# Joined 512-column matmuls, renumbered lags, idle matmuls at the start and a new order of operations in a one-core kernel

## The chip, the cores and the metric

The kernel runs on one core of one Trainium2 chip. The metric is the device time of one execution in microseconds (us). It is given as the median of several runs, with the range beside it. A profile is one of these executions; its span is about 2 us shorter than the device time of the same run. PE is the matmul engine, PEld its weight load, DVE the vector engine, ACT the scalar engine, POOL the general one, and SP the engine that issues most transfers. A line of a profile names an engine, a line of the kernel (L996), the operation and the tiles.

## The reference, cut to what matters

```python
def reference(A_u, ..., B_w_gate, B_w_up, B_w_down):      # u: 1 x 2048 x 512, bf16
    xn = layernorm(A_u)
    # A: per channel a kernel K of 2048 lags, as a sum over 128 modes, then a long convolution
    P = exp(dt * A * l)                                   # 512 channels x 128 modes x 2048 lags
    K = einsum("dn,dnl,dn->dl", C, P, dt * B).real
    y = irfft(rfft(pad(xn)) * rfft(pad(K)))[:L] + xn * Dskip
    # B: a gated network, 512 -> 1792 -> 512
    b = (sigmoid(xn @ w_gate) * (xn @ w_up)) @ w_down
    return A_u + y + b
```

The kernel takes the Fourier transforms apart into small matmuls. A table of 41 "lags" (powers of the complex modes) per channel quarter is made on DVE; matmuls turn it into K. A first stage transforms the input, a forward spectrum stage and a kernel spectrum stage follow, DVE multiplies the two spectra, and an inverse stage gives v, which is stored in DRAM. Then v is read back in another layout, and a last stage, S2, finishes the inverse transform. The gated network's matmuls run between all that.

## The kernel before

A list `ORDER` of 982 numbers fixes the order of all operations; each engine takes its own in that order. These are the parts that the change touches. The table's operations work on adjacent or on every second lag:

```python
powers(9, 2, 1, 2, 4, 3, [1, "3", "5"])       # results at lags 9, 11, 13, 15 from 1, 3, 5, 7
squares(10, 2, 5, 1, 3, ["5", "6"])
powers(17, 1, 2, 2, 7, 8, [2, 4, 8, "6", "10"])
powers(24, 2, 16, 2, 4, 9, [16, "17"])
# ... (cut)
def f_b():    # second half of a complex multiplication: L738, L739
    V.tensor_tensor(out=outp[:, :, :, 0, :], in0=outp[:, :, :, 0, :], in1=tb()[:, :, :, 1, :], op=opr)
    V.tensor_tensor(out=outp[:, :, :, 1, :], in0=outp[:, :, :, 1, :], in1=tb()[:, :, :, 0, :], op=opi)
```

The idle matmuls, whose results nobody reads, and the inverse stage (L939; the forward one, L898, is built alike), with two channel halves of DW = 256:

```python
keep_warm(14, -10)
for n in range(3):
    keep_warm(2, 1000 + n)
# ...
def fv(u=u, sv=sv, pp=pp, pq=pq):
    for y in range(2):
        src = ...                              # two or four operands
        for n, (z, q) in enumerate(src):
            for g in range(2):
                for b in (0, 64):
                    o = b ^ 64 * g
                    T.matmul(two(sv)[o:o + 64, DW * (2 * g + y):DW * (2 * g + y) + DW], mab[...],
                             z[b:b + 64, DW * g:DW * g + DW], ...)
```

And the end: the loads of v and S2. In each partition one tile t of one half p takes 2 KB, and the halves lie 16 KB apart:

```python
vps = [[at(16 * KB * p + 2 * KB * t, [2, 2, DW]) for t in range(8)] for p in range(NP)]
for t in range(8):
    for p in range(NP):
        lds.append(dma("SP" if p == 0 or t % 2 == 0 else "ACT", vps[p][t], v_v[:, :, 2 * t:2 * t + 2, :], ...))

def s2_mm(t, r, o, start, ps=(0, 1)):
    i = 2 * t + r
    for p in ps:
        for j in range(2):
            T.matmul(o[:, DW * p:DW * p + DW], s2[:, j, :], vps[p][t][:, j, r, :], ...)      # L996
        if i >= 12:
            T.matmul(o[:, DW * p:DW * p + DW], sr[:, i - 12, :], rr[:, DW * p:DW * p + DW], ...)
```

Of the kernel before, what the change touches and what calls it, by code (L numbers as in the profile page):

```python
# [13 lines left out]
ACT = mybir.ActivationFunctionType  # L14
# [22 lines left out]
NP, DW = 2, 256  # L37
# [17 lines left out]
LAG0 = (list(range(16)) + [256 + 2 * j for j in range(8)] + [768, 512, 772, 516, 776, 520, 780, 524]  # L55
        + [1024, 1280, 1288, 1792, 1800, 1536, 1544, 1032, 2048])
EXP = {6: 1, 10: 1, 12: 3, 14: 1, 19: 1, 21: 1, 22: 3, 23: 1, 27: 1, 29: 1, 31: 3, 30: 3, 37: 1, 38: 1, 39: 3}
# [117 lines left out]
def _consts():  # L175
# [30 lines left out]
UEV = (15, 19, 23, 24, 27, 28, 29, 30, 31, 32, 33, 34, 35, 36, 37, 38, 39, 40, 41, 42, 43, 44)  # L206
ON_ACT = (0,)
ORDER = [
    1, 0, 38, 28, 27, 37, 3, 4, 47, 2, 30, 29, 48, 50, 31, 49, 39, 52, 41, 51, 32, 14, 5, 7, 17, 10, 18, 6, 40, 34, 12, 42,
    33, 53, 35, 43, 44, 45, 24, 15, 94, 36, 638, 644, 93, 92, 46, 632, 54, 633, 639, 19, 105, 131, 645, 634, 95, 108, 640,  # L210
    59, 646, 685, 675, 134, 686, 132, 11, 676, 655, 656, 665, 58, 695, 670, 106, 666, 696, 96, 107, 671, 13, 16, 9, 660,
    690, 23, 677, 8, 118, 120, 119, 60, 97, 61, 98, 55, 62, 100, 691, 63, 101, 56, 678, 661, 121, 64, 680, 650, 137, 679,
    133, 21, 662, 135, 681, 651, 99, 57, 66, 672, 673, 109, 663, 635, 140, 102, 65, 67, 68, 664, 674, 179, 697, 138, 698,
    122, 636, 637, 699, 682, 667, 668, 687, 69, 20, 70, 683, 669, 684, 688, 71, 689, 149, 700, 647, 123, 110, 648, 701, 180,
    692, 72, 103, 652, 653, 22, 139, 136, 104, 111, 649, 693, 73, 124, 694, 654, 75, 113, 657, 141, 658, 150, 641, 702, 703,
    158, 642, 74, 659, 704, 728, 731, 76, 643, 181, 736, 77, 732, 227, 151, 142, 78, 127, 705, 182, 126, 183, 184, 738, 173,
    185, 739, 79, 186, 737, 706, 115, 707, 81, 80, 82, 83, 729, 733, 753, 754, 734, 708, 228, 740, 229, 230, 84, 85, 159,
    174, 175, 160, 187, 735, 87, 713, 231, 232, 86, 170, 88, 714, 125, 164, 773, 751, 90, 189, 233, 715, 112, 774, 165, 188,
    190, 166, 756, 171, 198, 192, 143, 199, 202, 200, 203, 752, 201, 755, 204, 757, 191, 206, 144, 193, 721, 167, 771, 205,
    741, 155, 772, 207, 722, 781, 172, 194, 709, 156, 145, 782, 742, 776, 152, 726, 783, 784, 777, 168, 208, 128, 114, 209,  # L220
    212, 785, 146, 723, 157, 169, 724, 727, 213, 725, 778, 779, 89, 153, 761, 763, 730, 780, 116, 764, 775, 762, 147, 129,
    154, 210, 788, 743, 91, 195, 216, 744, 214, 161, 148, 765, 758, 176, 215, 211, 745, 218, 196, 759, 760, 219, 217, 197,
    117, 234, 235, 766, 786, 177, 162, 787, 220, 222, 789, 790, 768, 716, 237, 245, 246, 236, 249, 274, 275, 250, 746, 239,
    238, 769, 767, 130, 247, 748, 770, 747, 749, 178, 163, 829, 849, 248, 276, 717, 240, 243, 750, 242, 253, 251, 241, 221,
    791, 432, 254, 433, 255, 223, 792, 402, 372, 256, 259, 224, 225, 434, 830, 226, 260, 261, 793, 244, 257, 794, 827, 403,
    373, 258, 262, 277, 438, 799, 252, 263, 850, 265, 266, 264, 404, 379, 436, 267, 374, 269, 278, 378, 408, 439, 268, 279,
    800, 283, 270, 847, 271, 280, 287, 284, 801, 281, 290, 286, 272, 292, 293, 282, 273, 440, 296, 321, 294, 297, 809, 848,
    435, 437, 371, 375, 851, 298, 828, 831, 322, 323, 857, 380, 295, 864, 441, 810, 409, 410, 300, 291, 442, 443, 301, 406,
    376, 381, 405, 377, 382, 394, 383, 395, 858, 288, 802, 285, 865, 867, 807, 396, 407, 302, 444, 303, 411, 808, 868, 289,
    387, 412, 388, 812, 817, 413, 389, 445, 424, 462, 469, 306, 832, 384, 818, 813, 391, 463, 304, 464, 837, 833, 838, 390,  # L230
    447, 392, 393, 859, 470, 385, 307, 299, 324, 819, 862, 811, 308, 860, 471, 397, 863, 398, 310, 499, 446, 468, 866, 305,
    465, 466, 386, 448, 414, 449, 467, 309, 312, 311, 313, 814, 822, 399, 415, 325, 417, 454, 400, 314, 823, 315, 820, 316,
    472, 473, 326, 861, 418, 336, 419, 331, 815, 317, 795, 327, 821, 852, 839, 455, 477, 416, 451, 452, 453, 450, 401, 484,
    425, 840, 853, 339, 328, 329, 872, 456, 426, 474, 421, 478, 854, 422, 841, 457, 340, 343, 873, 816, 458, 423, 420, 475,
    479, 476, 481, 855, 333, 824, 893, 483, 522, 480, 482, 341, 894, 332, 342, 825, 427, 335, 826, 344, 428, 485, 842, 334,
    843, 486, 459, 844, 345, 460, 347, 346, 856, 492, 898, 834, 845, 899, 835, 487, 488, 836, 803, 429, 430, 338, 523, 529,
    461, 348, 846, 349, 869, 900, 874, 524, 875, 870, 493, 489, 871, 494, 350, 876, 507, 901, 498, 527, 497, 431, 353, 895,
    905, 913, 354, 330, 318, 355, 490, 896, 351, 508, 357, 509, 491, 525, 513, 511, 512, 514, 352, 319, 337, 359, 903, 358,
    877, 356, 360, 320, 496, 526, 510, 361, 362, 363, 618, 364, 365, 528, 622, 620, 495, 369, 628, 878, 879, 366, 897, 367,
    906, 515, 953, 500, 516, 517, 880, 501, 530, 518, 604, 502, 885, 519, 531, 552, 503, 624, 553, 886, 887, 554, 532, 520,  # L240
    597, 598, 914, 559, 605, 904, 599, 954, 923, 533, 560, 888, 943, 589, 606, 561, 924, 537, 558, 534, 555, 556, 557, 562,
    563, 544, 603, 602, 538, 955, 928, 539, 535, 956, 564, 601, 600, 521, 957, 929, 545, 958, 918, 574, 607, 944, 565, 567,
    543, 504, 608, 536, 546, 542, 541, 582, 568, 540, 368, 547, 566, 959, 919, 569, 933, 934, 548, 907, 960, 908, 583, 630,
    505, 570, 571, 573, 609, 961, 584, 930, 572, 506, 931, 909, 610, 575, 576, 925, 549, 590, 962, 902, 616, 932, 586, 550,
    585, 587, 588, 611, 591, 926, 927, 577, 915, 945, 935, 578, 551, 579, 881, 592, 370, 889, 593, 580, 946, 916, 936, 937,
    594, 595, 581, 947, 950, 948, 596, 917, 612, 920, 626, 921, 949, 951, 963, 938, 952, 617, 922, 613, 625, 629, 940, 910,
    26, 941, 939, 614, 615, 619, 627, 911, 942, 631, 912, 964, 967, 710, 711, 965, 882, 712, 718, 968, 883, 966, 890, 623,
    884, 971, 969, 891, 719, 621, 804, 972, 970, 892, 796, 720, 975, 805, 797, 976, 977, 806, 798, 973, 978, 974, 25, 980,
    979, 981]
# [60 lines left out]
def kernel(  # L310
# [221 lines left out]
    keep_warm(14, -10)  # L532
    for n in range(3):
        keep_warm(2, 1000 + n)
# [4 lines left out]
    def layernorm(i0, i1, prio):  # L539
# [14 lines left out]
        for i in range(i0, i1):  # L554
# [20 lines left out]
            tr = pl.add("PE", 0.80, ft, [xn_ready[i - 1], xn_ready[i], l_id], prio, acq=[sl])  # L575
# [58 lines left out]
    q5 = pl.add("ACT", 2.15, f_sin, [q3, q4], PR, tab="sin")  # L634
# [85 lines left out]
    def cmul(lo, outp, n, m, conj, buf, deps, prio):  # L720
# [9 lines left out]
        def f_a():  # L730
            lov = wide(lo) if n == 1 or lo.ap[2][0] == 4 else lo
            ov = wide(outp) if n == 1 or outp.ap[2][0] == 4 else outp
            V.tensor_tensor(out=ov, in0=lov, in1=mre, op=ALU.mult)  # L733
            V.tensor_tensor(out=wide(tb()), in0=lov, in1=mim, op=ALU.mult)  # L734
# [5 lines left out]
        a = pl.add("DVE", 0.14 + 0.27 * n, f_a, deps, prio, acq=[sl])  # L740
        return pl.add("DVE", {1: 0.37, 2: 0.48, 4: 0.73, 7: 1.19}.get(n, 0.15 + 0.134 * n), f_b, [a], prio - 0.1, rel=[sl])
# [3 lines left out]
    for c in range(4):  # L745
# [26 lines left out]
        for dst, src in ((1, 0), (2, 1), (4, 2), (8, 3), (16, 8), (25, 9), (32, 10), (40, 11)):  # L772
            def f_s(H=H, dst=dst, src=src, c=c, ws=ws):
                S.activation(out=H[:, :, dst, :, :].rearrange("p r c h -> p c r h"),
                             in_=W[c // 2][:, src, :, ws].rearrange("p c (r h) -> p c r h", h=2), func=ACT.Identity)
            seeds[dst] = pl.add("ACT", 0.31, f_s, [W_op[src], cur_op] + hdep, PC)
# [5 lines left out]
        def powers(o0, os, l0, ls, nn, lev, need):  # L782
            h_ops[str(o0)] = cmul(H[:, :, l0:l0 + (nn - 1) * ls + 1:ls, :, :], H[:, :, o0:o0 + (nn - 1) * os + 1:os, :, :], nn,
                                  W[c // 2][:, lev, :, ws], False, "tg", dep(need) + [W_op[lev], o_g], PC - 0.5)
# [206 lines left out]
    def s2_mm(t, r, o, start, ps=(0, 1)):  # L991
        kw = dict(stop=True, skip_group_check=True)
        i = 2 * t + r
        for p in ps:
            for j in range(2):
                T.matmul(o[:, DW * p:DW * p + DW], s2[:, j, :], vps[p][t][:, j, r, :], start=start and j == 0, **kw)  # L996
# [150 lines left out]
```

## Time and profile before

| | before |
|---|---|
| time | 244.35 us, median of 3 runs (244.27 to 244.44) |
| span of the profiled run | 242.7 us |
| PE / DVE / ACT busy | 218.4 / 193.2 / 180.8 us |
| PE idle from 70 to 169 us | 6.7 us |
| last table matmuls start | 168.96 us |
| last inverse group ends | 212.54 us |

The prediction below shows the lines from which this is read. First the transfers that SP issues from 229 us on, then PE's timeline of the same stretch, then the row of PE's granted clock in 40 slices (9 is full). A timeline line has start, duration, engine, line, operation, result and operand, and the count merged into it; an idle time ahead of it would stand in brackets.

```profile
229.25 0.53 SPq L416 DMA_DIRECT2D big<-v_scr  x1
230.05 7.51 SPq L416 DMA_DIRECT2D out_dram<-big  x6
```

```profile
228.88 1.03 PE L996 MATMUL pair<-big 128*128 128x256 bf16 x8
229.75 3.19 PE L1076 MATMUL bank<-wd_sb,hT_sb 128*128 128x512 bf16 x13
232.78 1.04 PE L996 MATMUL pair<-big 128*128 128x256 bf16 x8
...
235.18 3.19 PE L1076 MATMUL bank<-wd_sb,hT_sb 128*128 128x512 bf16 x14
```

(The clock records of this profile begin at 17.50 us. What lies before the first record is counted as full, here and in every granted clock below, so a slow start doesn't show in them: twenty 256-column matmuls from 14.89 us took 180 ns each, ten from 117.62 us 109.)

### The profile page before, as it was taken

The numbers are of one execution on the slowest core, as the hardware profiler recorded it, in microseconds if no ns is written. First come the engines' busy times: TensorE is split into PE (matmuls) and PEld (weight loads), VectorE is DVE, ScalarE is ACT, GpSimd is POOL, SyncE is SP. The second block draws the span as 40 slices with busy tenths as digits, with TensorE's granted clock in tenths as the row PEclk, the third lists the DMA queues.
The fourth block names the chain that finished last, engine by engine and source line by source line (L and its number), as shares of the span: only waits on it lengthen the run. The fifth ranks groups of instructions, "written<-read, shape, count | busy, mean of one in ns | idle before, by whom it ended". The sixth has DMA issues, their size and how long they took to land.

```text
span 242.7 us, 5745 instructions
## 1 busy us (share of the span) xinstructions
PE 218.4 (90%) x2248; PEld 120.6 (50%) x2276; DVE 193.2 (80%) x397; ACT 180.8 (75%) x292; POOL 17.1 (7%) x42
## 2 busy tenths in 40 slices
PE   0099999999998999989989999999899999999994
PEld 0065444444443354555555575544564655644862
DVE  2997999999999999999999999999053246760662
ACT  3789999999999888848699999985555878440000
POOL 1303070001000020002010000000020100000000
PEclk9999999999999999999999999999999999999999
DMA  7999946501334896317975865625689798679262
GB/s 139 250 286 370 353 154 175 148 3 21 109 130 140 248 220 133 100 48 182 258 179 148 244 166 154 214 68 135 189 243 242 168 284 216 162 170 332 107 216 89
DMA packets 50861, 43.64 MB, mean 180 GB/s; under 512 B 12561, under 2 KB 44050, under 8 KB 50834
## 3 DMA queue, kind: packets, MB, share of 16 engines
q1 hardware_dynamic: 48738, 40.58, 58.8%
q0 software_dynamic: 864, 1.57, 4.1%
q10 hardware_dynamic: 1232, 1.11, 1.4%
q8 instruction: 18, 0.29, 0.5%
q14 instruction: 9, 0.07, 0.1%
HBM read 24.64 MB, written 12.06 MB: 151 GB/s over the span
## 4 chain that ended last, share of the span: by engine, by line
PE 35%; DVE 30%; ACT 23%; DMA 7%; issue 3%; SPq 1%; DVEq 0%; ACTq 0%
PE bank L1076 10%; PE bank L1028 6%; DVE big L733 5%; DVE big L734 5%; PE pair L916 5%; ACT big L666 4%; ACT big L672 4%; DVE big L739 4%; PE bank L1043 4%; DVE big L738 4%; ACT hT_sb L1037 3%; DVE hT_sb L1058 3%; ACT big L697 3%; PE pair L939 3%; ACT big L557 3%
## 5 line engine op out<-in xcount | busy, mean ns | idle before, releaser
L1028 PE MATMUL bank<-xnT,wg_sb 128*128 128x512 bf16 (+1 forms) x228 | 55.1, 375 | 2.3 <-issue 0.7
L1043 PE MATMUL bank<-xnT,wu_sb 128*128 128x512 bf16 x214 | 53.3, 379 | 2.0 <-DVE hT_sb L1058 1.1
L1076 PE MATMUL bank<-wd_sb,hT_sb 128*128 128x512 bf16 x216 | 50.3, 379 | 0.6 <-issue 0.2
L1028 PEld LDWEIGHTS <-wg_sb 128*128 128x128 bf16 x236 | 23.1, 100 | 27.4 <-issue 4.1
L1037 ACT ACTIVATE hT_sb<-bank 128x512 bf16<-128x512 f32 x56 | 32.1, 611 | 3.8 <-PE bank L1028 3.7
L1043 PEld LDWEIGHTS <-wu_sb 128*128 128x128 bf16 x224 | 21.1, 98 | 26.3 <-issue 3.4
L922 DVE TENSOR_TENSOR big<-big 128x2048 bf16<-128x2048 bf16 x16 | 19.5, 1222 | 18.3 <-PE pair L939 6.7
L1076 PEld LDWEIGHTS <-hT_sb 128*128 128x128 bf16 x224 | 21.4, 98 | 25.1 <-issue 0.4
L733 DVE TENSOR_TENSOR big<-big 128x1024 bf16<-128x1024 bf16 (+4 forms) x40 | 25.9, 647 | 0.9
L734 DVE TENSOR_TENSOR big<-big 128x1024 bf16<-128x1024 bf16 (+4 forms) x40 | 25.8, 644 | 0.0
L1058 DVE TENSOR_TENSOR hT_sb<-hT_sb,bank 128x512 bf16<-128x512 bf16 x34 | 22.4, 681 | 3.7 <-PE bank L1043 2.1
L916 PE MATMUL pair<-big 128*128 128x256 bf16 x160 | 19.8, 273 | 1.3 <-DMA big<-c_E 1.3
L918 ACT ACTIVATE big<-pair 128x1024 bf16<-128x1024 f32 x16 | 16.2, 1031 | 5.6 <-PE pair L916 5.0
L943 ACT ACTIVATE big<-pair 128x1024 bf16<-128x1024 f32 x16 | 16.4, 1035 | 4.5 <-DMA v_scr<-big 2.5
L738 DVE TENSOR_TENSOR big<-big 128x512 bf16<-128x512 bf16 (+4 forms) x40 | 18.8, 469 | 0.6
L739 DVE TENSOR_TENSOR big<-big 128x512 bf16<-128x512 bf16 (+4 forms) x40 | 18.5, 463 | 0.0
L916 PEld LDWEIGHTS <-big 128*128 128x128 bf16 x160 | 15.3, 98 | 6.0 <-DMA big<-c_E 1.6
L903 ACT ACTIVATE big<-pair 128x1024 bf16<-128x1024 f32 x16 | 16.3, 1027 | 1.7 <-PE pair L898 1.7
L697 ACT ACTIVATE big<-pair 128x1024 bf16<-128x1024 f32 x16 | 16.1, 1025 | 0.0
L790 ACT ACTIVATE sq_sb<-big 128x256 bf16<-128x256 bf16 (+2 forms) x20 | 12.7, 632 | 4.5 <-DVE big L796 3.1
L1054 ACT ACTIVATE us_sb<-bank 128x512 bf16<-128x512 f32 x22 | 13.0, 598 | 1.0 <-DVE hT_sb L1058 0.9
L666 ACT ACTIVATE big<-big 128x512 bf16<-128x512 f32 x24 | 13.8, 628 | 0.0
(106 smaller groups left out, 274.8 us busy)
## 6 DMA issues: line engine op xcount, KB each, us to landing
big<-c_E SPq DMA_DIRECT2D x16, 320.0 KB, 3.4
z_scr<-big SPq DMA_DIRECT2D x16, 256.0 KB, 2.7
big<-z_scr SPq DMA_DIRECT2D x16, 256.0 KB, 3.8
big<-big SPq DMA_DIRECT2D x64, 64.0 KB, 3.4
v_scr<-big SPq DMA_DIRECT2D x16, 256.0 KB, 3.2
big<-v_scr SPq DMA_DIRECT2D x12, 256.0 KB, 4.1
big<-in_A_u_dram SPq DMA_DIRECT2D x4, 512.0 KB, 5.8
wu_sb<-in_B_w_up_dram SPq DMA_DIRECT2D x2, 896.0 KB, 10.2
```

The costliest lines, as they stand in the source:

```text
L666: S.activation(out=W[p][:, k], in_=cur[:, :, DW * p:DW * p + DW], func=ACT.Identity)
L697: ev = pl.add("ACT", 0.90, lambda sl=sl, zs=zs: S.activation(out=zs().rearrange("p j d -> p (j d)"), in_=two(sl), func=ACT.Identity), [fx_ ...
L733: V.tensor_tensor(out=ov, in0=lov, in1=mre, op=ALU.mult)
L734: V.tensor_tensor(out=wide(tb()), in0=lov, in1=mim, op=ALU.mult)
L738: V.tensor_tensor(out=outp[:, :, :, 0, :], in0=outp[:, :, :, 0, :], in1=tb()[:, :, :, 1, :], op=opr)
L739: V.tensor_tensor(out=outp[:, :, :, 1, :], in0=outp[:, :, :, 1, :], in1=tb()[:, :, :, 0, :], op=opi)
L916: T.matmul(two(sk)[:, o:o + DW], es()[:, g, kt, :], kT[p][:, kt, :], start=kt in (0, NKT - 1), stop=kt >= NKT - 2)
L1028: T.matmul(bank(sl)[:, c0:c1], w[:, kt, k * 128:(k + 1) * 128], xnT[:, grp, kt, c0:c1], start=(kt == 0), stop=(kt == KT - 1))
L1037: S.activation(out=hT_sb[:, hs.idx, k % 2, :], in_=bank(sl), func=ACT.Sigmoid)
L1043: T.matmul(bank(sl), wu_sb[:, kt, k * 128:(k + 1) * 128], xnT[:, grp, kt, :], start=(kt == 0), stop=(kt == KT - 1))
L1058: V.tensor_tensor(out=h(), in0=h(), in1=us_sb[:, us.idx, :] if on else bank(sl), op=ALU.mult)
L1076: T.matmul(bank(po), hT_sb[:, hts[k // 2].idx, k % 2, jj * 128:(jj + 1) * 128], wd_sb[:, k, :], start=(k == 0), stop=k == FT - 1, **kw)
```

## The change

The intent: DVE writes table results to adjacent lags, short matmuls are joined into ones of 512 columns, PE is warmed up before its first real work, and the order is searched anew for these durations. The core of the diff:

```diff
-LAG0 = (list(range(16)) + [256 + 2 * j for j in range(8)] + [768, 512, ...] ...)
+LAG0 = [0, 1, 3, 5, 7, 6, 4, 2, 8, 10, 14, 12, 9, 11, 13, 15, 256, 262, ...]
-    keep_warm(14, -10)
-    for n in range(3):
-        keep_warm(2, 1000 + n)
+    warm = [keep_warm(14, -10)] + [keep_warm(4, -9 + n) for n in range(6)]
@@ (the first transposes get "+ warm" in their list of dependencies)
-        powers(9, 2, 1, 2, 4, 3, [1, "3", "5"])
-        squares(10, 2, 5, 1, 3, ["5", "6"])
-        powers(17, 1, 2, 2, 7, 8, [2, 4, 8, "6", "10"])
+        powers(12, 1, 4, 3, [1, "2", "3"])
+        squares(9, 3, 3, ["3", "5"])
+        powers(17, 5, 7, 8, [6, 7, 8, "5", "9"])
@@ (and so on: every result a run of adjacent lags)
@@ the inverse stage; the forward one likewise
-                T.matmul(two(sv)[o:o + 64, DW * (2 * g + y):DW * (2 * g + y) + DW], ...)
+                T.matmul(two(sv)[o:o + 64, DW * (2 * g + y):2 * DW * (g + 1)], ...)
@@ S2
-    vps = [[at(16 * KB * p + 2 * KB * t, [2, 2, DW]) for t in range(8)] for p in range(NP)]
+    vall = at(0, [NP, 8, 2, 2, DW])
+    vps = [[vall[:, p, t] for t in range(8)] for p in range(NP)]
-        for p in ps:
-            for j in range(2):
-                T.matmul(o[:, DW * p:DW * p + DW], s2[:, j, :], vps[p][t][:, j, r, :], ...)
+        w = slice(DW * ps[0], DW * ps[-1] + DW)
+        for j in range(2):
+            T.matmul(o[:, w], s2[:, j, :], vall[:, ps[0]:ps[-1] + 1, t, j, r, :], ...)
@@ ORDER: 985 numbers, a new sequence (cut)
@@ the estimates of durations for the search, the choice of engine for some evictions (cut)
```

## The prediction

> **What bounds the kernel now.** I read the page's busy shares first, then a table of engines by stretch, then who PE waited for, and last the timelines of PE and DVE. The page:
>
> ```profile
> PE 218.4 (90%) x2248; PEld 120.6 (50%) x2276; DVE 193.2 (80%) x397; ACT 180.8 (75%) x292; POOL 17.1 (7%) x42
> PE   0099999999998999989989999999899999999994
> DVE  2997999999999999999999999999053246760662
> ACT  3789999999999888848699999985555878440000
> ```
>
> PE does nothing in the first two slices and is near full in all others; DVE is full from slice 4 to slice 28 and slack after; ACT is full up to about 70 us. So no one engine bounds the whole. The stretches (columns: busy us of PE, PEld, DVE, ACT, POOL, then clock and DMA):
>
> ```profile
> 0.00:11.90 11.90, 0.00 (x0) 0.00 (x1) 6.91 (x25) 6.25 (x10) 2.93 (x12) 1.00 0.86 191
> 20.00:70.00 50.00, 49.55 (x226) 22.36 (x229) 47.28 (x102) 49.70 (x84) 6.29 (x13) 1.00 0.53 160
> 70.00:110.00 40.00, 36.74 (x476) 18.83 (x478) 39.31 (x87) 33.50 (x61) 1.22 (x3) 1.00 0.54 147
> 110.00:169.00 59.00, 55.57 (x746) 32.30 (x752) 58.65 (x120) 52.42 (x88) 2.44 (x6) 1.00 0.65 174
> 169.00:239.00 70.00, 68.46 (x764) 41.58 (x774) 32.52 (x48) 31.99 (x42) 2.27 (x3) 1.00 0.73 209
> ```
>
> Up to 70 us ACT (49.70 of 50) and PE are full together. From 70 to 169 us DVE is the full one (39.31 of 40, 58.65 of 59) and PE loses 3.26 + 3.43 = 6.7 us. From 169 us PE alone is full (1.5 us lost in 70). At the end there is nothing to win but PE work, since DVE and ACT are half idle; in the middle, DVE work is worth what PE loses by it. The waits of PE say how much that is:
>
> ```profile
> PE pair L573 <- DVE big L562: 11.9, 1, 11.9
> PE pair L822 <- DVE big L795: 1.7, 2, 1.2
> PE pair L916 <- DMA big<-c_E: 1.3, 1, 1.3
> PE bank L1043 <- DVE hT_sb L1058: 1.1, 1, 1.1
> PE pair L844 <- ACT big L828: 0.9, 1, 0.9
> ```
>
> 11.9 us are the start (loads and layernorm of the first tiles); of the rest, DVE table results and DVE products hold up PE most, but in small pieces. And the start on PE:
>
> ```profile
> 11.90 1.89 PE L573 MATMUL pair<-ident,big 128*128 128x128 bf16 x16 [11.90 <-DVE big L562]
> 13.58 1.06 PE L529 MATMUL bank<-glu_sb 128*128 128x512 bf16 x2
> 14.89 3.60 PE L1028 MATMUL bank<-xnT,wg_sb 128*128 128x256 bf16 x20 [0.24 <-ACT xnT L578]
> 26.53 3.19 PE L529 MATMUL bank<-glu_sb 128*128 128x512 bf16 x14
> ```
>
> Twenty 256-column matmuls take 3.6 us, 180 ns each, where 256 columns take 109 ns later (ten of L916 from 117.62 to the next start at 118.71): PE starts cold. The fourteen idle matmuls that were meant to warm it run at 26.5 us, when it has long been warm, as a filler of 3.0 us.
>
> [...] Trace: fourteen 512-column ones from 26.53 to 29.55 are 216 ns each, so joining by itself saves almost nothing. [...]
>
> ```profile
> 64.00 0.42 DVE L738 TENSOR_TENSOR big<-big 128x512 bf16<-128x512 bf16 x1
> 70.68 0.63 DVE L738 TENSOR_TENSOR big<-big 128x512 bf16<-128x512 bf16 x1
> 109.18 0.43 DVE L738 TENSOR_TENSOR big<-big 128x512 bf16<-128x512 bf16 x1
> 129.58 0.64 DVE L738 TENSOR_TENSOR big<-big 128x512 bf16<-128x512 bf16 x1
> ```
>
> 0.42 is a four-lag result with adjacent lags (the G table), 0.63 one with every second lag (the powers that start at lags 9 and 24).
>
> **The change part by part.**
>
> (1) Lags renumbered. Number and sizes of the table operations per channel quarter stay: powers of 1, 2, 4, 7, 4, 4 lags, squares of 1, 3, 3, 2, 1. Only the add/subtract halves (L738, L739) and the two instructions of each square (L795, L796) gain; the multiplies L733 and L734 take 0.69 us at 1024 elements either way. By start-to-start time of the pair L738 and L739: a power of four lags takes 1.08 us stepped (70.68 to 71.76) and 0.67 adjacent (64.00 to 64.67), so two of them save 0.82; the power of two lags, 0.39 + 0.38 us stepped against 0.30 + 0.28 adjacent in the same timeline, saves 0.19;[...] the seven-lag power was adjacent already. Sum 0.82 + 0.19 + 0.12 = 1.13 us a quarter, four quarters 4.5 us of DVE, nearly all between 67 and 169 us where DVE is full. PE loses 6.7 us in that stretch; not all to DVE (1.3 us is a DMA, 0.9 + 0.5 ACT). I take 3.0 us as shortening the whole, the rest as DVE time that PE has no idle time to give back.
>
> (2) Idle matmuls. All 38 (14 + 6 x 4) now go ahead of the first transpose, from about 1.4 us (the memset that they read ends at 0.85 + 0.52). [...] what follows runs warm. From 14.89 to 21.35 PE does 24 matmuls of 256 columns and 11 of 512, which are 24 x 0.109 + 11 x 0.216 = 5.0 us warm in 6.46 us: 1.5 us lost; the 16 transposes take 1.9 us[...]. ACT is close to full from 15 us and takes part of this back: I count 1.5 us. The fillers at 26.5 us go, but PE stood there for ACT's evictions (ACT 49.70 of 50), so nothing is counted; the two fillers at 218 us lie in the PE-bound end and free 0.4 us.
>
> (3) Joined matmuls. The inverse spectrum stage (L939) goes from 24 of 256 to 8 of 512 and 8 of 256, four array tiles at a time: 0.68 us a block now (125.06 to 125.74)[...]. The forward one (L898) goes from 8 to 4 matmuls: 0.32 us a block now (125.74 to 126.06)[...]. The last stage (L996), 64 of 256 to 32 of 512[...]. [...]I count 0.7, as the first half lies where DVE is full.
>
> (4) Order and small moves. Two tiles' statistics go to ACT instead of one (0.85 us less DVE, about 1.5 us more ACT, early where ACT is idle), one eviction fewer on ACT. The order of all 985 operations is new; it decides how much of (1) and (2) arrives. I expect it to be good, and count nothing.
>
> Sum: 3.0 + 1.5 + 0.4 + 0.7 = 5.6 us, 244.35 - 5.6 = 238.7 us.
>
> **The rivals.** (a) PE is the bound all along and DVE time is hidden: PE lost only 6.7 us in the DVE stretch, and the 70 us at the end are PE work that a faster table doesn't shorten. Then only (2) and (3) count, 2.6 us, and the time is 241.7. For it: the last 74 us are dense PE; against it: the table waits of L822 and the bank waits on DVE. (b) DVE is the bound up to 169 us and the end follows it: all 4.5 us plus the 0.85 of the statistics arrive, and the start 1 us earlier as well: 236 us. For it: DVE at 58.65 of 59; against it: work that PE doesn't do by then it must do after. (c) The idle matmuls end after the transposes are ready and hold up the whole start by 1 us, and a first weight load that lands later (the order moves the first gate piece back) adds to it: 241. For it: 38 matmuls are a fixed cost in order on PE; the first gate now waits 0.9 us for its weights. (d) The new order trades one wait for another, E-table loads or ACT evictions: 240 to 243.
>
> **Range and chances.** The middle is 238.7. Rivals (a), (c) and (d) pull up by 2 to 4 us, (b) pulls down by 3; so 235.5 to 242.3 eight times in ten. The border of 2% is 239.5, close to the middle: faster by over 2% 0.57, within 2% 0.41, slower by over 2% 0.02, as nothing added lies on PE after the start.
>
> **What would show it.** (1) L738 and L739 at 512 elements all near 0.42 us, mean of the group 0.42 to 0.45 instead of 0.53, DVE's sum down by 4 to 5 us, and the last quarter's table matmuls (L822, now from 168.96) starting 4 to 6 us earlier. (2) Idle matmuls from 1.4 to about 12 us, L1028 at 256 columns near 270 ns instead of 345 on average, the first gate near 14 us. (3) L939 blocks at 0.65 to 0.68 us, so hardly changed. (4) PE's idle time between 70 and 169 us down from 6.7 to below 4. If that idle time stays while DVE's sum falls, step (1) was worth nothing; if a new wait of over 1 us stands among PE's waits, rival (d); if the transposes start after 12.5 us waiting for PE itself, rival (c).

The sum of this forecast was 3.0 + 1.5 + 0.4 + 0.7 = 5.6 us, 244.35 to 238.7. Where the marks stand, terms and grounds are cut that no trace or run of this case shows. In step (1) the squares of three lags are 0.12 of the 1.13 us a quarter; 0.82 + 0.19 = 1.01 are from traces. In step (3) the 0.7 counted there is a bare guess. What the trace shows for it is 109 ns for a matmul of 256 columns against 216 for one of 512, so a saving of about 2 ns a pair.

## More of the kernel before

```profile
PEclk9999999999999999999999999999999999999999
```

A load of v is issued at 229.25 us, S2 runs at 232.78 us with no bracket, so PE did not stand before it, and the clock stays full to the end.

## The result, and the profile after

| | before | after |
|---|---|---|
| time, same chip | 244.39 us (244.27 to 244.57, 4 runs) | 248.03 us (247.13 to 248.68, 4 runs) |
| ratio of after to before | | 1.0146 (95% interval 1.011 to 1.0182) |
| span of the profiled run, granted clock | 242.7 us, 1.000 | 246.7 us, 0.979 |

Ratios here and below are the mean time of one kernel's fast runs over that of the other's fast runs in the same rounds, so not quite the ratio of the medians beside them. The changed kernel is 3.6 us slower, where the prediction had 5.6 us faster. It also scatters more: 1.6 us between its runs against 0.3. By the ratio it is 1.5% slower. That lies within the 2% either way to which the prediction gave 0.41, but on the side that it did not expect.

The page of the changed kernel, busy sums and rows:

```profile
PE 228.5 (93%) x2069; PEld 114.9 (47%) x2069; DVE 187.3 (76%) x397; ACT 181.5 (74%) x295; POOL 17.4 (7%) x42
PE   7959999989999998999999999999999996999492
DVE  3997999999999999999999999940635454516324
PEclk9979999999999999999999999999999999799979
```

DVE has 5.9 us less to do, as intended. PE is full for longer, yet has holes in the last seven slices, and the clock row has a 7 at three places: near 15, 210 and 235 us. The clock records behind the row show 0.50 from 15.21, 209.77 and 233.66 us, for 3.41 us each; I call that half clock. The same stretches as in the prediction (busy us of PE, PEld, DVE, ACT, POOL, then clock and DMA):

```profile
70.00:110.00 40.00, 38.55 (x536) 19.82 (x535) 39.15 (x90) 35.54 (x68) 2.47 (x6) 1.00 0.68 166
110.00:169.00 59.00, 58.51 (x780) 32.49 (x779) 52.79 (x116) 51.50 (x84) 1.76 (x4) 1.00 0.63 167
169.00:239.00 70.00, 63.54 (x438) 31.11 (x437) 30.07 (x42) 29.74 (x38) 1.73 (x2) 0.95 0.67 191
```

From 70 to 169 us PE is idle for 1.45 + 0.49 = 1.9 us instead of 6.7, and the last quarter's table matmuls start at 162.71 us, 6.2 us earlier. From 169 us on it is idle for 6.5 us instead of 1.5, at a lower clock. So the gain of the middle came, and the end lost more. The adjacent table results, by size (busy us, mean ns):

```profile
L734 DVE TENSOR_TENSOR big<-big 128x512 bf16<-128x512 bf16 x16 | 7.0, 436 | 0.1
L735 DVE TENSOR_TENSOR big<-big 128x512 bf16<-128x512 bf16 x16 | 6.9, 430 | 0.0
```

The means were 533 and 526 ns, when half of the sixteen were adjacent already. What PE now waits for (us in total, times, longest):

```profile
PE pair L992 <- DMA big<-v_scr: 4.1, 3, 3.1
PE pair L934 <- DVE big L917: 2.4, 1, 2.4
PE pair L693 <- ACT xnT L576: 1.7, 1, 1.7
...
PE bank L1024 <- DMA wg_sb<-in_B_w_gate_dram: 1.2, 1, 1.2
```

L992 is S2, L934 the inverse stage, L917 a product of spectra. Neither of the first two waits stood among the long ones of the kernel before. The end, first what SP issues, then PE:

```profile
226.92 0.52 SPq L416 DMA_DIRECT2D big<-v_scr  x1
227.54 1.79 SPq L416 DMA_DIRECT2D out_dram<-big  x2
231.34 0.53 SPq L416 DMA_DIRECT2D big<-v_scr  x1
```

```profile
226.73 3.19 PE L1072 MATMUL bank<-wd_sb,hT_sb 128*128 128x512 bf16 x14
230.27 1.04 PE L992 MATMUL pair<-big 128*128 128x512 bf16 x4 [0.36 <-DMA big<-v_scr]
234.44 1.89 PE L992 MATMUL pair<-big 128*128 128x512 bf16 x4 [3.13 <-DMA big<-v_scr]
```

Between two S2 groups of four matmuls PE stands for 3.13 us, waiting for the load that SP issued at 231.34 us. And that load had waited in turn for S2: among SP's waits from 219 us on there is one that the kernel before doesn't have.

```profile
SPq L416 <- PE pair L992: 3.2, 2, 1.9
```

That is a chain in which a load waits for a read and the next read waits for the load. By the order of the program the load of 231.34 us brings tile 0 of the second half. The two groups of S2 around it are those of tiles 4 and 2. Neither needs tile 0.

The theory that I took from this: in this kernel, the waits between reads and writes of that buffer follow the stretch of addresses from the first to the last byte that an instruction touches. The joined read of tile 2 begins at tile 2 of the first half and ends at tile 2 of the second. Tile 0 of the second half lies in between, untouched but inside. I call such a wait a false wait. The rivals: the idle start and its half clock cost most of it (1.7 + 1.2 us of waits), or joining in itself costs, as a joined group needs both halves' loads, or the new order is simply bad at the end.

### The profile page after: what moved, and what is told of

Its sections match the earlier page's. It is cut to its first block, busy times and chain, and to the rows that moved or that the text cites. A ratio compares the mean times of both kernels' runs of the same rounds, so it can differ in the third digit from the quotient of the medians.

```text
span 246.7 us, 5371 instructions
## 1 busy us (share of the span) xinstructions
PE 228.5 (93%) x2069; PEld 114.9 (47%) x2069; DVE 187.3 (76%) x397; ACT 181.5 (74%) x295; POOL 17.4 (7%) x42
## 4 chain that ended last, share of the span: by engine, by line
PE 58%; ACT 15%; DMA 13%; DVE 5%; SPq 4%; issue 2%; ACTq 1%; DVEq 0%
PE bank L1024 14%; PE bank L1039 13%; PE bank L1072 10%; PE pair L911 7%; DMA big<-v_scr 5%; PE pair L934 5%; PE pair L818 3%; ACT hT_sb L1033 3%; PE pair L992 3%; ACT big L695 3%; DMA z_scr<-big 3%; DMA wg_sb<-in_B_w_gate_dram 2%; SPq L416 2%; ACT big L664 2%; ACT big L670 2%
## 5 line engine op out<-in xcount | busy, mean ns | idle before, releaser
L1024 PE MATMUL bank<-xnT,wg_sb 128*128 128x512 bf16 (+1 forms) x236 | 56.0, 376 | 1.2 <-DMA wg_sb<-in_B_w_gate_dram 1.2
L1039 PE MATMUL bank<-xnT,wu_sb 128*128 128x512 bf16 x224 | 56.1, 384 | 0.1
L1072 PE MATMUL bank<-wd_sb,hT_sb 128*128 128x512 bf16 x224 | 51.3, 382 | 0.8 <-ACT glu_sb L1102 0.6
L1033 ACT ACTIVATE hT_sb<-bank 128x512 bf16<-128x512 f32 x56 | 33.1, 615 | 6.6 <-PE bank L1024 6.6
L1054 DVE TENSOR_TENSOR hT_sb<-hT_sb,bank 128x512 bf16<-128x512 bf16 x35 | 23.3, 680 | 9.2 <-PE bank L1039 9.1
L917 DVE TENSOR_TENSOR big<-big 128x2048 bf16<-128x2048 bf16 x16 | 19.5, 1219 | 11.9 <-DMA big<-v_scr 3.8
L938 ACT ACTIVATE big<-pair 128x1024 bf16<-128x1024 f32 x16 | 16.5, 1031 | 5.4 <-DMA v_scr<-big 3.5
L898 ACT ACTIVATE big<-pair 128x1024 bf16<-128x1024 f32 x16 | 16.4, 1032 | 4.9 <-PE pair L893 3.9
L913 ACT ACTIVATE big<-pair 128x1024 bf16<-128x1024 f32 x16 | 16.5, 1034 | 2.0 <-PE pair L911 1.2
L734 DVE TENSOR_TENSOR big<-big 128x512 bf16<-128x512 bf16 (+4 forms) x40 | 16.8, 420 | 0.2
L695 ACT ACTIVATE big<-pair 128x1024 bf16<-128x1024 f32 x16 | 16.9, 1074 | 0.0
L735 DVE TENSOR_TENSOR big<-big 128x512 bf16<-128x512 bf16 (+4 forms) x40 | 16.6, 416 | 0.0
L934 PE MATMUL pair<-big 64*64 64x512 bf16 (+1 forms) x256 | 14.1, 339 | 2.4 <-DVE big L917 2.4
L664 ACT ACTIVATE big<-big 128x512 bf16<-128x512 f32 x24 | 14.1, 654 | 0.0
L786 ACT ACTIVATE sq_sb<-big 128x256 bf16<-128x256 bf16 (+2 forms) x20 | 13.2, 663 | 1.0 <-DVE big L735 0.8
```

The source lines that it names most:

```text
L664: S.activation(out=W[p][:, k], in_=cur[:, :, DW * p:DW * p + DW], func=ACT.Identity)
L695: ev = pl.add("ACT", 0.90, lambda sl=sl, zs=zs: S.activation(out=zs().rearrange("p j d -> p (j d)"), in_=two(sl), func=ACT.Identity), [fx_ ...
L917: V.tensor_tensor(out=pp().rearrange("p q h m -> p (q h) m"), in0=xx().rearrange("p q h m -> p (q h) m"), in1=kb()[:, 0:2 * DW].unsqueeze( ...
L934: T.matmul(two(sv)[o:o + 64, DW * (2 * g + y):2 * DW * (g + 1)], mab[b:b + 64, 2 * u + g, q, :], pq()[b:b + 64, q, ch] if y else pp()[b:b ...
L1024: T.matmul(bank(sl)[:, c0:c1], w[:, kt, k * 128:(k + 1) * 128], xnT[:, grp, kt, c0:c1], start=(kt == 0), stop=(kt == KT - 1))
L1033: S.activation(out=hT_sb[:, hs.idx, k % 2, :], in_=bank(sl), func=ACT.Sigmoid)
```

## The experiments

"Before" below is always the kernel before, run beside each experiment on the same chip: 244.63 us (243.75 to 245.89, 7 runs) in the first four, 244.42 (244.15 to 246.35, 7 runs) in the second four, 244.31 (243.51 to 245.33, 11 runs) in the last four. The first four were, in the order of this section, the first four below; the second four are the tile-by-tile buffer, the two joins, the first try without idle matmuls and the bridge; the last four are the rest. Each four ran on a chip of its own. All results were correct.

### Reading the halves apart in the changed kernel

```diff
-        for j in range(2):
-            T.matmul(o[:, w], s2[:, j, :], vall[:, ps[0]:ps[-1] + 1, t, j, r, :], ...)
+        for p in ps:
+            for j in range(2):
+                T.matmul(o[:, DW * p:DW * p + DW], s2[:, j, :], vps[p][t][:, j, r, :], ...)
```

> The changed kernel with one thing undone: the last spectrum stage (S2) reads its two channel halves by separate 256-column matmuls from separate views again. Theory 1: the joined read spans both halves of the buffer, so a load of one tile's second half has to wait for matmuls of other tiles (in the program two of the last loads wait on PE; in this kernel they don't), and PE then waits for those loads: PE's waits on v_scr loads fall from 4.1 us to below 2, the half-clock window at 234 us goes, the time falls by 2 to 4 us to 244 to 246. Theory 2: the tail is late because of the order of loads and stores on the sync queue alone: no change, 247.5 to 248.5.

Measured: 242.50 us (240.76 to 243.21), ratio to before 0.9906 (0.9855 to 0.9957). Everything else of the change is still in. The same two S2 groups, now sixteen short matmuls:

```profile
226.18 3.19 PE L1071 MATMUL bank<-wd_sb,hT_sb 128*128 128x512 bf16 x14
229.20 1.91 PE L991 MATMUL pair<-big 128*128 128x256 bf16 x16
230.95 3.19 PE L1071 MATMUL bank<-wd_sb,hT_sb 128*128 128x512 bf16 x14
```

No wait between them. PE's waits for loads of v fall from 4.1 us to 1.9, one wait before the first of these groups. The joined S2 is thus worth some 5.5 us of loss (248.03 to 242.50, on two chips), more than the 2.2 us by which these waits fell. Part of the rest is half clock: in the changed kernel the four joined matmuls at 234.44 us took 1.89 us, as long as the eight at 222.84 us. The granted clock of the four runs is 0.976 to 0.982 in the changed kernel and 0.986 to 0.992 here; times the spans that is 2.7 us of lost work, my estimate. Not all of it comes from S2. The changed kernel has two half-clock stretches near the end, each of 3.41 us by the clock records. The one at 233.66 us follows S2's wait. The one at 209.77 us follows the wait for the products (L934), which is still here, 2.8 us long, but was not followed by half clock in this profile: the sixteen matmuls after it took 1.01 us, against 1.49 in the changed kernel.

### The first gate weights earlier

```diff
@@ ORDER: load 10 (first piece of the gate weights) moved ahead of load 11 (second piece)
```

> The changed kernel with one load moved in the order: the first piece of the gate weights is issued before the second piece, the S1 constant and the two tiles' parameters, instead of after them. Theory 1: in the changed kernel PE runs dry from 12.4 to 15.9 us for these weights and drops to half clock for 3.4 us from 15.2; with the weights there at 12 to 13 us, the first gate matmul starts near 14.6 us, the half-clock window there goes or moves, and the time falls by 1.5 to 3 us to 245 to 246.5. Rival: ACT is full from 15 to 70 us and sets the pace, so the earlier start is given back: less than 0.5 us.

Measured: 247.22 us (245.88 to 247.84), ratio 1.0102 (1.0057 to 1.0147). PE's wait for gate weights is gone, the wait for ACT's copy of the transposes became 2.0 us, and the half clock at 15 us stayed (the granted clock from 11.9 to 20 us is 0.79, as in the changed kernel). Some 0.8 us (1.1 by the ratios), with overlapping intervals: the late weights are not the main cause.

### All three joins in the kernel before

```diff
@@ the kernel before, with the joined forward, inverse and S2 matmuls of the change; lags, idle matmuls and order as before
```

> The kernel before with all three joined stages and nothing else. Theory 1 (joined matmuls save columns' overhead only, 0.7 us): 243.4 to 244.2. Rival (the joined S2 read adds waits between loads and matmuls of different tiles): one load waits on PE that didn't before, 244.5 to 247, with a new PE wait on v_scr loads.

Measured: 248.69 us (247.81 to 249.67), ratio 1.0171 (1.0122 to 1.0219). The joins alone make the old kernel as slow as the whole change, in an order that did not suffer before:

```profile
235.30 1.89 PE L996 MATMUL pair<-big 128*128 128x512 bf16 x4 [3.09 <-DMA big<-v_scr]
```

That is the group which ran at 232.78 us without a wait. It belongs to tile 3. Here it is the load that waits falsely. ACT issues four loads of v, the last of them the second half of tile 3, which this group does need. Before, then in this run:

```profile
219.14 3.38 ACTq L416 DMA_DIRECT2D big<-v_scr  x4
```

```profile
218.45 11.31 ACTq L416 DMA_DIRECT2D big<-v_scr  x4
```

By the trace the fourth went out at 221.90 us before. Now it goes out at 229.22, released by an S2 matmul, and lands at 235.26. The S2 group just ahead of it in the order is that of tile 5, which doesn't need tile 3, but whose stretch covers it. A half-clock stretch follows PE's wait, 234.93 to 238.34 us: the four matmuls at 235.30 us took 1.89 us, the four at 224.26 us 1.03. It is not the whole loss: the run with a granted clock of 0.998, which lost almost nothing to half clock, still took 247.81 us.

### The renumbered lags in the kernel before

```diff
@@ the kernel before, with LAG0, powers() and squares() of the change; the old order, each operation held until what it needs is issued
```

> The kernel before with the renumbered lags alone (its order kept, apart from table operations held back until what they now need is there). Prediction's step 1: DVE falls by 4 to 4.5 us and the time by 2 to 4 us, to 240.5 to 242.5. Rival (PE is the bound all along): DVE falls as much, the last quarter's table is earlier, the time stays within 1 us of 244.4.

Measured: 259.15 us over all four runs (256.53 to 261.51; two of them, over 1.5% above the fastest, count as slow), ratio 1.0518 (1.0461 to 1.0575). DVE's sum falls to 190.5 us, but PE waits for the table:

```profile
PE pair L819 <- DVE big L735: 6.1, 2, 3.2
PE pair L819 <- ACT hT_sb L1034: 2.8, 2, 1.8
PE bank L1025 <- DVE hT_sb L1055: 2.6, 1, 2.6
```

This missed its purpose. The new numbering makes the table a longer chain of results that need each other, with squares on ACT in between, and the old order blocks the engines on it: by the lists of what each result needs, the chain is 8 results deep instead of 6. That this is what costs the time is my reading of the waits. The lags have no value apart from an order made for them, so I count lags and order as one term from here on.

### The joined read over a buffer laid out tile by tile

```diff
-    vall = at(0, [NP, 8, 2, 2, DW])
-    vps = [[vall[:, p, t] for t in range(8)] for p in range(NP)]
+    vall = at(0, [8, NP, 2, 2, DW])
+    vps = [[vall[:, t, p] for t in range(8)] for p in range(NP)]
-            T.matmul(o[:, w], s2[:, j, :], vall[:, ps[0]:ps[-1] + 1, t, j, r, :], ...)
+            T.matmul(o[:, w], s2[:, j, :], vall[:, t, ps[0]:ps[-1] + 1, j, r, :], ...)
```

This is the changed kernel with the joins in, and no tile of another number between the two halves of one.

> The changed kernel with one edit: the loaded v lies tile by tile (tile, half, ...) instead of half by half, so that the joined 512-column read of a tile covers that tile's two loads only. Theory (the false waits come from the stretch of addresses that the joined read spans, not from joining): no wait of a v load on the joined matmuls, the wait of 3.1 us before the last joined group is gone, the page says full clock in the last 15 us, and the time is 241.5 to 243.0, that is as in the run with the halves read apart (242.5), within 0.5 us of it. Rival (the joined matmul itself, or the joined wait for both halves, holds up the end): a wait of over 2 us before the joined group stays, time 245 or more.

Measured: 241.90 us (241.42 to 242.73), ratio 0.9878 (0.9827 to 0.9929). What SP issues, and PE:

```profile
224.56 0.52 SPq L416 DMA_DIRECT2D big<-v_scr  x1
226.22 2.07 SPq L416 DMA_DIRECT2D out_dram<-big  x2
228.34 0.53 SPq L416 DMA_DIRECT2D big<-v_scr  x1
```

```profile
228.70 1.89 PE L992 MATMUL pair<-big 128*128 128x512 bf16 x8
230.43 3.19 PE L1072 MATMUL bank<-wd_sb,hT_sb 128*128 128x512 bf16 x14
```

S2 starts 0.36 us after the same load was issued, and these loads took 4.2 us from issue to landing (median of this page), so it cannot have waited for it. All eight joined matmuls run in one piece. SP has no wait for S2 any more. So in this kernel it is not the joining, nor the one name `vall`, which this version keeps, but the stretch of addresses that the joined read spans. That is settled by this run (241.90 us) together with the first (242.50). The runs show which waits come and go with the layout; how the waits are set was not looked at.

### Two of the joins in the kernel before

```diff
@@ the kernel before, with the joined forward and inverse matmuls; S2 as before
```

> The kernel before with the joins of the forward (four 512-column instead of eight 256-column) and inverse spectrum matmuls alone, S2 as it was. By the prediction's step 3 [...]243.4 to 244.3 against 244.4 for the kernel before. Theory (the loss of the run with all three joins, +4.1 us, is from S2 alone): not slower than before, ratio 0.996 to 1.000, no new wait at the end. Rival (joining holds banks or operands longer in these stages too): over 1 us slower, ratio above 1.004.

Measured: 244.89 us (244.46 to 246.23), ratio 1.0016 (0.9967 to 1.0065). No loss, and no gain that could be seen; the 0.7 us of the prediction are within what this doesn't tell apart from nothing.

### S2 alone joined in the kernel before

```diff
@@ the kernel before, with s2_mm() and vps of the change
```

> The kernel before with the joined S2 matmuls alone, in the half-by-half layout. Theory (all of the loss of the three joins together, 248.7, is from here): 247.5 to 249.0, a wait of about 3 us for a load of v and a half-clock window of 3.4 us behind it. Rival (the loss needs the other joins too): under 246.

Measured: 246.76 us (246.59 to 247.29), ratio 1.0095 (1.0062 to 1.0128).

```profile
231.76 1.46 PE L1077 MATMUL bank<-wd_sb,hT_sb 128*128 128x512 bf16 x6
235.39 1.04 PE L997 MATMUL pair<-big 128*128 128x512 bf16 x4 [2.17 <-DMA big<-v_scr]
```

The loss is here, 2.4 us, about the wait, but less than I expected: no half clock followed it, and the granted clock is 1.000 in all four runs. As with all three joins, ACT's load of tile 3's second half went out late, at 230.44 us. With all three joins the wait was longer, 3.09 against 2.17 us, and half clock followed it. That may be why this loss and the 0.4 us of the other two joins fall short of the 4.1 us of all three; it was not tested, and the three ran on three chips.

### Without the idle matmuls

```diff
-    warm = [keep_warm(14, -10)] + [keep_warm(4, -9 + n) for n in range(6)]
+    warm = [keep_warm(2, -10)] + [keep_warm(0, -9 + n) for n in range(6)]
```

First on the version with halves read apart:

> The changed kernel with S2's halves read apart (242.5) and 36 of its 38 idle matmuls at first taken out, two left. The prediction gave the warm start 1.5 us. Theory (the warm-up is lost in the idle 3 us after the transposes, as the half clock at 16.6 to 20.0 shows, so it gains little): 242.3 to 243.2, no more than 0.7 us slower than with the matmuls, possibly even as fast, for the transposes no longer wait for them. Rival (prediction's step 2, 1.5 us): 243.8 or more.

Measured: 244.77 us over four runs (242.23 to 246.82), ratio 0.9967 (0.9896 to 1.0039). By this my guess of at most 0.7 us was too low, but the runs were wide apart. So I ran the tile-by-tile version with and without, in five rounds:

> The tile-by-tile version again, in five rounds, as the partner of the next two: 241.4 to 242.7. Its runs differ more than those of the kernel before[...]: over 1 us between its fastest and slowest run is expected.

> The tile-by-tile version without 36 of the 38 idle matmuls at first. The first try of this on the version with halves read apart (244.8, between 242.2 and 246.8) spoke against my guess of no more than 0.7 us. If the warm start is worth the prediction's 1.5 us or more: 243.4 to 244.5. [...]within 0.7 us of the partner, 242 to 243.

Measured: with idle matmuls 242.66 us (241.52 to 244.43, 6 runs), ratio 0.9932 (0.9894 to 0.997); without 243.58 us (242.29 to 245.59, 6 runs), ratio 0.9973 (0.9934 to 1.0012). The difference is 0.9 us between the medians and 1.0 between the means of six and six runs. Worked out from these runs, its 95% interval goes from 0.5 us the other way to 2.5 us, so neither nothing nor the predicted 1.5 us is excluded, and of my two expectations neither is settled. (The second, within 0.7 us, was meant for the case that the first try's slow runs were chance.) The runs of one batch scatter more in the mended variants, by 1.3 to 4.6 us, than in the kernel before, by 0.3 to 2.2. Mostly the slower runs have the lower granted clock (tile by tile without idle matmuls from 242.29 us at 0.998 to 245.59 at 0.988), but not always: the slowest of the first four tile-by-tile runs, 242.73 us, had the highest, 0.996. Why a run falls to half clock and another doesn't was not shown. The profiles show what the idle matmuls change. In the two tile-by-tile ones the transposes start at 11.46 us with them and at 10.16 without, but the sixteen then take 2.17 us instead of 1.06, so that they end at 12.52 and 12.33 us. The start of the version with halves read apart, without them:

```profile
11.37 1.03 PE L571 MATMUL pair<-ident,big 128*128 128x128 bf16 x8 [1.07 <-DVE big L560]
14.10 1.01 PE L693 MATMUL pair<-big 128*128 128x512 bf16 x2 [1.69 <-ACT xnT L576]
16.38 6.49 PE L1023 MATMUL bank<-xnT,wg_sb 128*128 128x256 bf16 x24 [1.28 <-DMA wg_sb<-in_B_w_gate_dram]
```

And of the changed kernel, with all of them:

```profile
1.43 10.11 PE L529 MATMUL bank<-glu_sb 128*128 128x512 bf16 x38 [1.43 <-POOL glu_sb L522]
11.37 1.06 PE L571 MATMUL pair<-ident,big 128*128 128x128 bf16 x16
14.16 0.59 PE L693 MATMUL pair<-big 128*128 128x512 bf16 x2 [1.74 <-ACT xnT L576]
15.93 5.80 PE L1024 MATMUL bank<-xnT,wg_sb 128*128 128x256 bf16 x24 [1.18 <-DMA wg_sb<-in_B_w_gate_dram]
```

With the idle matmuls or without, PE stands from about 12.4 to 14.1 us for ACT's copy of the transposes, and again for weights. The changed kernel has full clock from 4.97 us, where its records begin, and half clock from 15.21 to 18.62 us. So do three of the four other profiles with these idle matmuls and no more at the start, at other times (with halves read apart and with the gate weights first the granted clock from 11.9 to 20 us is 0.79, as here); the first one of the tile-by-tile version kept 1.00 up to 205 us, after waits of 0.86, 1.36 and 0.49 us.

### Bridging the wait at the start

```diff
@@ the tile-by-tile version; load 10 ahead of load 11; 8 more idle matmuls right after the transposes
+    keep_warm(8, -8)
```

> The tile-by-tile version with two more edits at the start: the first gate weight piece is issued before the second, and 8 more idle matmuls stand between the transposes and the wait for their copy (1.7 us at full clock). If the clock is lost because PE sits idle there, no half-clock window before 30 us, and PE's first 60 matmuls take about 1.7 us less; if ACT sets the pace up to 70 us the end gains less: 241.0 to 242.3. Rival (the window comes anyway, or the bridging matmuls delay the gate): same as the tile-by-tile version or slower.

Measured: 242.40 us (240.33 to 243.14), ratio 0.9891 (0.9829 to 0.9953). No half clock before 200 us: the granted clock is 1.00 up to 205. That by itself shows little, as the parent's profile beside it had none there either. But PE's wait for ACT's copy of the transposes, 0.86 us in the parent and 1.74 in the changed kernel, is gone; up to 24 us the timeline shows one wait after the transposes, 1.43 us for gate weights before 18.53 us. So the bridge fills the wait that it was made for. The time is that of its parent all the same (0.9878 beside it, 0.9932 in the later runs). Less idle time at the start doesn't bring the end forward by an amount that shows here, which fits ACT setting the pace up to 70 us (busy for 49.85 of the 50 us from 20 to 70); that it is ACT was not tested by itself.

### The last inverse group later

```diff
@@ the version just above; ORDER: the last inverse group, its eviction and its store moved behind the next two groups of the up projection
```

> The version with the gate piece earlier and the idle matmuls between the transposes and their copy (242.4), with the last inverse group moved behind the next two groups of the gated network, so that PE works while the products that it waits for (1.9 to 2.8 us) are made. If that wait lies on the path to the end: no wait of PE for the products of over 0.5 us, no half clock after 200 us, 239.5 to 241.2. Rival (the end follows the store and load of v, which the move doesn't bring forward): 241.5 to 242.5 with the wait turned into one for the loads of v.

Measured: 244.76 us over six runs (243.09 to 246.91), ratio 0.9998 (0.9959 to 1.0036): some 2 us worse than its parent, by the fast runs too. The profile fell in a run of the slow state (246.91 us), so only the kind of its waits is used, and what follows is a reading and not shown for the fast runs. PE, and DVE before them:

```profile
PE pair L992 <- DMA big<-v_scr: 3.2, 1, 3.2
PE bank L1039 <- DVE hT_sb L1054: 2.9, 1, 2.9
```

```profile
207.64 1.23 DVE L917 TENSOR_TENSOR big<-big 128x2048 bf16<-128x2048 bf16 x1 [2.72 <-DMA big<-big]
208.78 0.69 DVE L921 TENSOR_TENSOR big<-big 128x1024 bf16<-128x1024 bf16 x1
209.38 2.48 DVE L1054 TENSOR_TENSOR hT_sb<-hT_sb,bank 128x512 bf16<-128x512 bf16 x4
```

DVE stands 2.72 us for a transfer ahead of the product, and the gated network's products (L1054), behind it in `ORDER`, start at 209.38 us; so PE waits for these instead, 2.89 us. The wait only changed its name. And the last part of v is stored later (213.07 us instead of 212.04 with the bridge alone), so S2 waits for its load. This is the rival of the expectation, and more.

## Why the prediction was wrong

**Step (3), the joined matmuls, failed.** The prediction counted 0.7 us for it, and only a small part of that for S2. It did not look at the new operand as a range of addresses with loads landing inside it. In place of a gain S2 brought a loss of some 5.5 us at the end, in false waits and half clock, as the halves read apart (242.50 us) and the tile-by-tile buffer (241.90 us, then 242.66) show against 248.03. The other two joins measured 0.4 us slower by the ratio, with an interval from 0.8 us faster to 1.6 us slower.

**The sentence "nothing added lies on PE after the start", on which the 2% for slower rested, was the same oversight.** Added waits lie on PE like added work, and here at the end, where PE alone was full (idle for 1.5 us of the 70 from 169 us on before).

**Step (1) was right in kind.** DVE saved 5.9 us where 4.5 and, in step (4), 0.85 for the statistics were predicted. By size: results of 512 elements (97 + 96) ns x 16 = 3.1 us as predicted; the squares of three lags, 510 and 526 ns to 385 and 381, (125 + 145) ns x 8 = 2.2 us, where it had allowed 0.5. The table matmuls came 6.2 us earlier, and PE's idle time in the stretch fell to 1.9 us, as it said (below 4). Its 3.0 us of arrival were too many. It had left room for 0.9 us of waiting for ACT (L844), but that wait ends at 172.57 us, outside the stretch. With the false waits away and without the idle matmuls, what is left is lags, order, joins and the small moves together: ratio 0.9973, 0.7 us, and the interval goes from 1.6 us faster to 0.3 slower, so nothing at all is within it and 3.0 us are not. Where it went can be followed in the version with halves read apart: the last inverse group ends at 210.31 us against 212.54, so 2.2 us of the 6.2 arrive there, and PE stands 2.8 us for the products just before. DVE, which makes them, had stood 2.51 us for a transfer (208.02 us), and a table that is done sooner doesn't bring that transfer. The attempt to work around this wait turned it into two others. That these products are the only thing that keeps the rest is not shown.

**Step (2) was wrong in "what follows runs warm".** The idle matmuls end at 11.5 us as it said (about 12). What follows is a wait of 1.7 us for ACT and 1.2 us for weights, and half clock from 15.21 us. Where there was none, as with the bridge, the end came no earlier by an amount that could be seen. The size is not settled: for the warm start's 1.5 us some 0.9 were measured, not clear of noise either way. The 0.4 us for the fillers were not measured alone; they are in the 0.7 us above, as all versions lack them.

**Rival (d)**, that the new order trades one wait for another, named the form of the result, but not its size ("240 to 243") nor its cause: the old order has the same wait once S2 is joined, and the new order loses it once the halves are read apart. Rival (c) was right in that the gate's weights came later (15.93 us for the first gate matmul instead of 14.89), worth some 0.8 us, not clear of noise, and in that the idle matmuls hold up the transposes (11.46 us instead of 10.16), which then make up most of it (1.06 us for the sixteen instead of 2.17). The 236 us of rival (b) don't follow from its own terms: 4.5 + 0.85 + 1 us off 244.35 are 238.0.

In the last batch the change with its layout mended is 1.6 us faster than the kernel before: 0.9 for the idle matmuls and 0.7 for all else, of which only the whole is clear of noise. Two of its forms, the tile-by-tile buffer (0.9878 and 0.9932) and the halves read apart (0.9906), beat both the kernel before, by about 1%, and the changed one.

## What to carry to other kernels

When two operands are joined into one access, look at everything that lies between their first and last byte, and at who writes it meanwhile: lay the joined parts side by side first, then join. A new wait for a load whose data the waiting instruction doesn't read, or a load that waits for a matmul which doesn't read what it overwrites, is the sign of it in a profile. Here a read with a jump of 16 KB waited for loads into the bytes that it jumps over, 3.13 us at one place, and held up such loads in turn (3.2 us in two waits), some 5.5 us in all with the half clock; with the same joined matmuls over an adjacent layout neither wait was there. And look at what follows idle matmuls at the start: here waits of 1.0 to 2.0 us after the transposes were followed by half clock in four profiles of five, and filling the wait moved the end by nothing that could be seen.
